# Second products of two token groups in float32, and a later split of w_out

## The chip, the cores and the metric

The kernel runs on one core of a Trainium2 chip. Its engines work side by side: TensorE (PE, matmuls, with its weight loads shown apart as PEld), VectorE (DVE), ScalarE (ACT), GpSimd (POOL) and SyncE (SP, which here only issues transfers). The metric is the device time of one execution in microseconds. The kernel before took 1150.65 us, the median of three runs (1146.93 to 1151.56).

## The reference

Attention with a causal mask and a bias from cumulative sums, for 8 batches of 8 heads, 576 positions, head dimension 64; then a gated feed-forward layer over the 4608 tokens of 512 numbers:

```python
scores = scale * np.matmul(q, k.transpose(0, 1, 3, 2))
cum = np.cumsum(np.maximum(s, 0.0), axis=-1)
bias = -(cum[:, :, :, None] - cum[:, :, None, :])
scores = np.where(causal, -1e9, scores + np.minimum(bias, 0.0))
attn = softmax(scores);  x = (attn @ v), heads side by side   # 4608 x 512
gate = 1.0 / (1.0 + np.exp(-(x @ w_gate)))                    # w_gate, w_val: 512 x 1536
out = (gate * (x @ w_val)) @ w_out                            # w_out: 1536 x 512
```

The weights arrive as 64-bit floats and are decoded on the chip to float32.

## The kernel before

Most products are made of float16 halves: each operand is scaled by a power of two and split into a high and a low half, and a product is the three passes high x high, high x low and low x high, added up in PSUM.

**Attention** goes head by head, five row tiles a head; one tile is a tick of the main loop (320 ticks). Scores are made on PE, bias and row bound on DVE (L529), the exponential on ACT (L530), the split of the result on ACT and DVE (L534, L539, L547), then DMA transposes it, and PE multiplies with v (L562 to L567). After each pair of heads the result is split and transposed into the tokens x of one batch. The first eight heads are done in float32, scores and product with v alike (L631, L662).

**The feed-forward layer** takes tokens in 18 groups of GT = 256 and the 1536 hidden columns in NF = 12 blocks f of 128. A unit (g, f) is `ffn_in`: 24 passes for gate and value (L714), the tanh on ACT (L719), and the gated product on DVE (L721). `ffn_mid` scales the product by `hsc` and splits it (L729 on ACT, L730 on DVE). `ffn_out` adds for both row tiles of 128 tokens the product with block f of w_out (L745, 512 columns) in PSUM, over f from 0 to 11, and after the last block copies the sum out with a scale (L764) and stores it (L765).

**The first two groups** are special. Their 24 units are issued in program order at ticks 44 to 51, while weights are still being decoded, and their gated products are kept in float32 (`t2first`, in the large buffer `t2big`). The scale `hsc` needs the sizes of all blocks of w_gate and of w_out, so their `ffn_mid` and `ffn_out` come only after `hidden_scale`, behind all 24 units.

**Weights** come in 18 steps: 12 for the blocks of w_gate and w_val, 6 for pairs of blocks of w_out. A step loads, decodes (L298 to L301), bounds the columns with a small matmul (L310, L313), makes a power-of-two scale `wscale` (L332, L334) and splits into halves (L337 on ACT, L338 on DVE). `invw` is the inverse of the scale. The halves of w_out lie in `w2all`, whose room also serves as raw room for loads.

**The last two groups** use fewer products: `tail_weights` builds sums of weight blocks (L787 to L795) in the rooms `troom`, `tail_tokens` sums of tokens, and `tail_pair` makes both groups' hidden values from seven half-depth products (L833), with copies and sums on ACT and DVE between (L846 to L864). Their `ffn_out` follow one block behind; those of block 11 come last, each row tile evacuated in halves by ACT and DVE (L755, L757).

**Order.** A planner fixes each engine's order of instructions before the run, from priorities (mostly program order), data dependencies and its own estimate of durations. On the chip each engine runs that order and waits where a dependency is late. Attention has raised priority (`first`) from tick 44 to 87, so weight steps, units and products of the first two groups fill what it leaves. From tick 87 on, units and attention are interleaved in program order; a group's units can start when all heads of its batches are done, and its `ffn_out` run LAG = 3 units behind.

Of the kernel before, what the change touches and what calls it, by code (L numbers as in the profile page):

```python
# [18 lines left out]
P = 128  # L19
GT = 256  # L20
# [5 lines left out]
def tile_attention_then_gated_ffn(  # L26
# [60 lines left out]
    w1 = [cp.tile([P, NC, 2, 2, P], F16, name=f"w1_{f}") for f in range(NF)]  # L87

    w2all = cp.tile([P, NF // 2, 2, 8, 2, DM // 8], F16, name="w2all")
    w2 = [w2all[:, f // 2, :, :, f % 2] for f in range(NF)]  # L90
    e_s = [cp.tile([P, n * P], F32, name=f"e_{i}") for i, (_, _, n) in enumerate(SETS)]
    p_s = [cp.tile([P, 2, n * P], F16, name=f"p16_{i}") for i, (_, _, n) in enumerate(SETS)]

# [39 lines left out]
    wscale = cp.tile([P, 2, NF], F32, name="wscale")  # L133
    hsc = cp.tile([P, NF], F32, name="hsc")
    gmax = cp.tile([P, 1], F32, name="gmax")
    cum_d = dp.tile([NH, S], F32, name="cum_d")

    def pin(ins):
# [177 lines left out]
    def split_weight(n, a, m):  # L316

        o, f = wsteps[n]
        if o:
            hi, lo = (w2all[:, f // 2, l].rearrange("p h x n -> p (h x n)") for l in range(2))  # L320
        else:
            a = a.rearrange("p (c n) -> p c n", n=P)
            hi, lo = (w1[f].rearrange("p c g l n -> p (c g) l n")[:, :, l] for l in range(2))
        if m is None:
            ss = wp.tile([P, 1], F32, tag="wss", name=f"wss{n}")
            nc.scalar.activation(hi, a, AF.Square, accum_out=ss)
            tot = wp.tile([P, 1], F32, tag="wst", name=f"wtot{n}")
            nc.gpsimd.partition_all_reduce(tot, ss, P, ADD_REDUCE)
            pow2_of(wscale[:, o, f : f + 1 + o], tot, f"w{n}", 204 if o else 202)
        else:  # L330
            e = wp.tile([P, 1], I32, tag="xe", name=f"xe_w{n}")
            nc.vector.tensor_scalar(e, column_bound(n, m).bitcast(I32), 0x7F800000, None, ALU.bitwise_and)  # L332
            dst = wscale[:, o, f : f + 1 + o]
            nc.vector.tensor_scalar(dst.bitcast(I32), e.to_broadcast([P, 2]) if o else e, -1.0,  # L334
                                    (268 if o else 266) * 2.0 ** 23, ALU.mult, ALU.add)
        sc = wscale[:, o, f : f + 1]
        nc.scalar.activation(hi, a, AF.Copy, scale=sc)  # L337
        nc.vector.scalar_tensor_tensor(lo, a, sc, hi, ALU.mult, ALU.subtract)  # L338

    def inverse_weights(o, fs):  # L340
        inverse_pow2(invw[:, o, fs], wscale[:, o, fs])

    def hidden_scale():


        inverse_weights(1, slice(0, NF))
        g = wp.tile([P, NF], F32, tag="hsg", name="hsg")
        nc.vector.tensor_tensor(g, invw[:, 0], invw[:, 1], ALU.mult)
        m = wp.tile([P, 1], F32, tag="hsm", name="hsm")
        nc.vector.tensor_reduce(m, g, mybir.AxisListType.X, ALU.max)  # L350
        nc.vector.tensor_scalar(gmax, m, 2.0 ** -100, None, ALU.max)
        r = wp.tile([P, 1], F32, tag="hsr", name="hsr")
        nc.vector.reciprocal(r, gmax)
        nc.vector.tensor_scalar(hsc, g, r, 2.0 ** -13, ALU.mult, ALU.mult)
        out_scale(0)

    osc = {}
# [347 lines left out]
    def ffn_in(g, f):  # L705
        pcs, n = pieces_of(g)
        ps = pp.tile([P, 2, GT], F32, tag="gv", name=f"gv{g}_{f}")
        for gv in range(2):
            for a, e, b in pcs:
                c0 = PAD + g * GT - b * S  # L710
                c = 0
                for cc in range(NC):
                    for wl, xl in ((0, 0), (0, 1), (1, 0)):
                        nc.tensor.matmul(ps[:, gv, a:e], w1[f][:, cc, gv, wl], x_of(b, cc)[:, xl, c0 + a : c0 + e],  # L714
                                         start=(c == 0), stop=(c == 3 * NC - 1))
                        c += 1
        th = fp.tile([P, GT], F32, tag="th", name=f"th{g}_{f}")
        for a, e, b in pcs:
            nc.scalar.activation(th[:, a:e], ps[:, 0, a:e], AF.Tanh, scale=scb[b][:, f : f + 1])  # L719
        t2 = t2first[g * NF + f] if g < 2 else fp.tile([P, GT], F32, tag="t2", name=f"t2_{g}_{f}")  # L720
        nc.vector.scalar_tensor_tensor(t2[:, :n], th[:, :n], 1.0, ps[:, 1, :n], ALU.add, ALU.mult)  # L721
        t2s[g, f] = t2
        if g > 1:
            ffn_mid(g, f)

    def ffn_mid(g, f):
# [5 lines left out]

    def ffn_out(g, f, tiles=range(GT // P), last=False):
        pcs, n = pieces_of(g)
        if g < 2:
            ffn_mid(g, f)
        h = hst[g, f]
        for tt in tiles:
            m = min(P, n - tt * P)
            if f == 0:  # L740
                tag = ("x", "av")[tt] if g == NG - 1 else "o"
                ops_[g, tt] = pp.tile([P, 512], F32, tag=tag, name=f"o{g}_{tt}", **({} if tag == "o" else {"bufs": 1}))
            ps = ops_[g, tt]
            for c, (hl, wl) in enumerate(((0, 0), (0, 1), (1, 0))):
                nc.tensor.matmul(ps[:m], h[:, hl, tt * P : tt * P + m], w2[f][:, wl],  # L745
                                 start=(f == 0 and c == 0), stop=(f == NF - 1 and c == 2))
            if f == NF - 1:
                i = (g * GT // P + tt) % 2
                o = rows_out[:, i * DM : (i + 1) * DM] if g < NG - 1 else last_rows(tt)
                if last:  # L750

                    b = pcs[-1][2]
                    rows = out[g * GT + tt * P : g * GT + tt * P + m, :]
                    w = DM // 2
                    nc.scalar.activation(o[:m, :w], ps[:m, :w], AF.Copy, scale=osc[b][:m])  # L755
                    nc.scalar.dma_start(rows[:, :w], o[:m, :w])
                    nc.vector.tensor_scalar(o[:m, w:], ps[:m, w:], osc[b][:m], None, ALU.mult)  # L757
                    nc.sync.dma_start(rows[:, w:], o[:m, w:])
                    del ops_[g, tt]
                    continue  # L760
                for a, e, b in pcs:
                    a, e = max(a - tt * P, 0), min(e - tt * P, P)
                    if a < e:
                        nc.scalar.activation(o[a:e], ps[a:e], AF.Copy, scale=osc[b][a:e])  # L764
                nc.gpsimd.dma_start(out[g * GT + tt * P : g * GT + tt * P + m, :], o[:m])  # L765
                del ops_[g, tt]

# [8 lines left out]
    G1, G2 = NG - 2, NG - 1  # L776
    GX = PAD + G1 * GT - (B - 1) * S
    TS, Sx = {}, {}
    troom = [t2big[:, i * 4 * GT : (i + 1) * 4 * GT] for i in range(6)]
    troom += [e_s[1][:, : 4 * GT], p_s[1].rearrange("p l n -> p (l n)").bitcast(F32)[:, : 4 * GT]]  # L780

    def tail_weights(f):
# [14 lines left out]

    def tail_tokens():

        a = t2big[:, 4 * 4 * GT : 6 * 4 * GT].rearrange("p (k c n) -> p k c n", k=4, n=GT)  # L800
        for k in range(4):
            for c in range(2):
                x_ = x_of(B - 1, 2 * (k % 2) + c)[:, :, GX + (k // 2) * GT : GX + (k // 2 + 1) * GT]
# [14 lines left out]
    def tail_pair(f):  # L818
# [10 lines left out]
        def product(ps, ws, xs, first_):  # L829
            c = 0  # L830
            for cc in range(NC // 2):
                for wl, xl in ((0, 0), (0, 1), (1, 0)):
                    nc.tensor.matmul(ps, ws[:, cc, wl], xs[cc][:, xl], start=first_ and c == 0, stop=c == 3 * NC // 2 - 1,  # L833
                                     skip_group_check=True)
                    c += 1

        ga = pp.tile([P, 2, GT], F32, tag="gv", name=f"ta{f}")[:, 0]
        un = pp.tile([P, 2, GT], F32, tag="gv", name=f"tu{f}")[:, 0]
# [13 lines left out]
        nc.vector.tensor_tensor(u2, un, one, ALU.add)  # L852
        product(ga, w[:, hi, 0], x(G1, 1), False)
        product(vd[:, 0], w[:, hi, 1], s(1), False)
        product(vd[:, 1], t[:, hi, 0], x(G2, 1), False)
        nc.vector.tensor_tensor(v2, five[:, 0], five[:, 1], ALU.add)
        nc.vector.tensor_tensor(v2, v2, u2, ALU.add)
        nc.vector.tensor_tensor(v1, vd[:, 0], u2, ALU.add)
# [1 line left out]
        for g, gate, val in ((G1, ga, v1), (G2, g2, v2)):  # L860
            th = fp.tile([P, GT], F32, tag="th", name=f"th{g}_{f}")
            nc.scalar.activation(th, gate, AF.Tanh, scale=scb[B - 1][:, f : f + 1])
            t2 = fp.tile([P, GT], F32, tag="t2", name=f"t2_{g}_{f}")
            nc.vector.scalar_tensor_tensor(t2, th, 1.0, val, ALU.add, ALU.mult)  # L864
            t2s[g, f] = t2
            ffn_mid(g, f)

    units = [(g, f) for g in range(NG) for f in range(NF)]
    state = {"u": 0, "o": 0}
# [29 lines left out]
    for n in range(nticks + 12):  # L899
# [146 lines left out]
        if n >= NE and state["u"] < 2 * NF:  # L1046
# [13 lines left out]
            if state["u"] == 2 * NF:  # L1060
                hidden_scale()
                while state["o"] < 2 * NF:
                    emit_out()
                late_slots()
        if (n - 30) % (NTL * H) == 0 and n >= 30 + NTL * H:
            ffn_scale((n - 30) // (NTL * H))
# [7 lines left out]
            while state["u"] < min(want, len(units)):  # L1074
                emit_unit()
    rest = len(units) - 2 * NF
    for f in range(4):
        tail_weights(f)
    tail_tokens()
    for f in range(4, len(troom)):  # L1080
        tail_weights(f)
    with first():
        while state["u"] < rest:
            emit_unit()
    for f in range(NF):
        tail_pair(f)
        while state["o"] < rest:
            emit_out()
        if f:
            ffn_out(G1, f - 1)  # L1090
            ffn_out(G2, f - 1)
        if f + len(troom) < NF:
            tail_weights(f + len(troom))
    for g in (G1, G2):
# [30 lines left out]
```

## Time and profile before

| | us |
|---|---|
| median of three runs | 1150.65 (1146.93 to 1151.56) |
| the profiled execution | 1149.97 |
| its span, first to last instruction | 1148.2 |
| PE busy in the span | 1092.8 (95%) |
| DVE busy | 828.9 (72%) |
| ACT busy | 753.4 (66%) |
| POOL busy | 203.1 (18%) |
| products with w_out (L745), 1296 matmuls, PE busy | 315.2 |

The profile is of one execution. A row of instructions gives start or count, busy time, the mean of one in nanoseconds, and the idle time of the engine just before, with what ended it. PE's ends are modelled and overlap from one matmul to the next, so spacing from start to start is the better measure of a matmul's cost. A row can carry several shapes.

### The profile page before, as it was taken

How to read it: one execution, taken by the hardware profiler on the slowest of the kernel's cores; microseconds unless marked ns; L12 is line 12 of the kernel's file. 1: busy time of each engine (PE TensorE's matmuls, PEld its weight loads, DVE VectorE, ACT ScalarE, POOL GpSimd, SP SyncE). 2: the span in 40 equal slices, each digit the busy share in tenths (PEclk: the TensorE clock that was granted, in tenths of full speed). 3: DMA queues.
4: the chain of work that ended last, by engine and by line, in shares of the span. 5: the costliest groups of instructions: out<-in, count | busy, mean ns of one | idle time of the engine just before them, and what ended most of it. 6: DMA issues, size and time to landing. Idle time of an engine off the chain costs nothing.

```text
span 1148.2 us, 30316 instructions
## 1 busy us (share of the span) xinstructions
PE 1092.8 (95%) x11796; PEld 856.6 (75%) x11796; DVE 828.9 (72%) x2360; ACT 753.4 (66%) x1475; POOL 203.1 (18%) x471
## 2 busy tenths in 40 slices
PE   6997868989999999999999999999999999999997
PEld 4776757747777787788777777778877787787775
DVE  6868979866787687766565567777777779673854
ACT  6878657767786777676656577767776766343433
POOL 3311101022232222221111122222221213000000
PEclk9999989999999999999999999999999999999999
DMA  9767886998989698875736468878877664100001
GB/s 281 226 183 140 195 151 142 179 182 166 172 170 174 156 177 162 154 151 116 170 66 149 99 156 162 162 156 169 165 146 158 142 118 95 23 20 11 10 1 37
DMA packets 445933, 157.62 MB, mean 137 GB/s; under 512 B 403615, under 2 KB 436383, under 8 KB 445790
## 3 DMA queue, kind: packets, MB, share of 16 engines
q1 hardware_dynamic: 418974, 127.64, 56.7%
q10 hardware_dynamic: 23616, 17.30, 5.2%
q0 software_dynamic: 3200, 10.75, 2.6%
q8 instruction: 92, 1.51, 0.5%
q14 instruction: 51, 0.42, 0.1%
HBM read 56.92 MB, written 9.58 MB: 58 GB/s over the span
## 4 chain that ended last, share of the span: by engine, by line
PE 70%; DMA 9%; DVE 7%; ACT 5%; issue 5%; SPq 2%; POOL 1%; ACTq 0%; DVEq 0%; POOLq 0%
PE gv L714 34%; PE o L745 20%; DMA v<-in_v_dram 3%; PE s L491 3%; PE tv L833 3%; PE s L489 3%; DMA T<-qk 1%; PE ta L833 1%; PE av L564 1%; DMA w2all<-in_moe_w_out_dram 1%; PE av L562 1%; DVE e L529 1%; PE av L563 1%; PE na_ps L662 1%; SPq L463 1%
## 5 line engine op out<-in xcount | busy, mean ns | idle before, releaser
L714 PE MATMUL gv<-x,w 128*128 128x256 f16 (+3 forms) x6336 | 555.6, 245 | 10.1 <-DVE t2f L721 6.7
L714 PEld LDWEIGHTS <-w 128*128 128x128 f16 x6336 | 481.7, 99 | 63.6 <-issue 11.7
L745 PE MATMUL o<-w2all,h 128*128 128x512 f16 x1296 | 315.2, 379 | 3.6 <-ACT h L729 3.5
L530 ACT ACTIVATE e<-e,em 128x576 f32<-128x576 f32 x280 | 153.3, 557 | 90.3 <-DVE em L529 87.5
L745 PEld LDWEIGHTS <-h 128*128 128x128 f16 x1296 | 123.2, 98 | 110.3 <-ACT h L729 5.2
L511 POOL TENSOR_SCALAR_AFFINE_SELECT rl<-rl 128x128 f32<-128x128 f32 (+1 forms) x240 | 89.7, 374 | 501.9 <-DVE em L529 460.1
L529 DVE CUSTOM_DVE_ANT_0 e<-s,rl,qkcf 128x576 f32<-128x576 f32 x280 | 151.3, 544 | 32.7 <-PE s L491 17.0
L729 ACT ACTIVATE h<-t,hsc 128x256 f16<-128x256 f32 x192 | 96.6, 503 | 91.0 <-DVE t L721 89.0
L719 ACT ACTIVATE th<-gv,scb 128x256 f32<-128x256 f32 (+3 forms) x264 | 99.1, 403 | 66.3 <-PE gv L714 59.0
L539 DVE SCALAR_TENSOR_TENSOR p<-e,p 128x384 f16<-128x384 f32 x224 | 102.9, 498 | 40.0 <-ACT p L534 38.3
L721 DVE SCALAR_TENSOR_TENSOR t<-th,gv 128x256 f32<-128x256 f32 x168 | 69.7, 415 | 63.8 <-ACT th L719 63.8
L730 DVE SCALAR_TENSOR_TENSOR h<-t,hsc,h 128x256 f16<-128x256 f32 x192 | 93.4, 487 | 28.7 <-ACT h L729 26.3
L534 ACT ACTIVATE p<-e 128x1152 f16<-128x1152 f32 x112 | 112.0, 1001 | 2.8 <-DMA pt<-p 0.3
L489 PE MATMUL s<-T 128*128 128x288 f16 (+2 forms) x246 | 63.8, 277 | 8.0 <-DMA T<-qk 4.1
L562 PE MATMUL av<-v,pt 128*128 128x65 f16 x560 | 67.6, 193 | 2.0 <-DMA pt<-p 2.0
L451 POOL PARTITION_BROADCAST cr<-cr x63 | 59.4, 950 | 56.8 <-DMA cr<-cum_d 33.2
L563 PE MATMUL av<-v,pt 128*128 128x64 f16 x560 | 67.6, 192 | 0.0
L564 PE MATMUL av<-v,pt 128*128 128x65 f16 x560 | 67.6, 194 | 0.0
L491 PE MATMUL s<-T 128*128 128x288 f16 (+2 forms) x246 | 61.5, 277 | 4.3 <-DMA T<-T 4.3
L562 PEld LDWEIGHTS <-pt 128*128 128x128 f16 x560 | 52.5, 97 | 7.8 <-DMA pt<-p 2.9
L563 PEld LDWEIGHTS <-pt 128*128 128x128 f16 x560 | 52.5, 97 | 4.5
L564 PEld LDWEIGHTS <-pt 128*128 128x128 f16 x560 | 52.7, 97 | 0.2
(210 smaller groups left out, 1542.4 us busy)
## 6 DMA issues: line engine op xcount, KB each, us to landing
v<-v SPq DMA_DIRECT2D x56, 162.5 KB
v<-in_v_dram SPq DMA_DIRECT2D x64, 128.0 KB
out_dram<-io POOLq DMA_DIRECT2D x32, 256.0 KB, 3.4
T<-T SPq DMA_DIRECT2D x82, 72.0 KB
t2f<-in_v_dram SPq DMA_DIRECT2D x20, 288.0 KB
qk<-in_q_dram SPq DMA_DIRECT2D x17, 288.0 KB
qk<-in_k_dram SPq DMA_DIRECT2D x17, 288.0 KB
w2all<-in_moe_w_gate_dram ACTq DMA_DIRECT2D x7, 512.0 KB
```

The source lines that it names most:

```text
L489: nc.tensor.matmul(ps[:, : b_ - a], lhs, T[i][:, 0, a:b_], start=True, stop=False)
L529: nc.vector.tensor_tensor_reduce(e, ps, r, c, MASKED, ALU.add, ALU.min, acc)
L530: nc.scalar.activation(e_t[t][:, :w], e_t[t][:, :w], AF.Exp, bias=acc, scale=-1.0)
L534: nc.scalar.activation(p_s[h_][:, 0], e_s[h_], AF.Copy, scale=PSCALE)
L539: nc.vector.scalar_tensor_tensor(flat[:, LOW[t] * P : (LOW[t] + t) * P], e_t[t][:, : t * P], PSCALE, flat[:, kb * P : (kb + t) * P], ALU.m ...
L562: nc.tensor.matmul(AV[i][:, t], hi, v_[:, D : 2 * D + 1], start=kb == 0, stop=False)
L563: nc.tensor.matmul(AV[i][:, t, 0:D], hi, v_[:, 0:D], start=False, stop=False)
L564: nc.tensor.matmul(AV[i][:, t], lo, v_[:, D : 2 * D + 1], start=False, stop=False)
L714: nc.tensor.matmul(ps[:, gv, a:e], w1[f][:, cc, gv, wl], x_of(b, cc)[:, xl, c0 + a : c0 + e], start=(c == 0), stop=(c == 3 * NC - 1))
L719: nc.scalar.activation(th[:, a:e], ps[:, 0, a:e], AF.Tanh, scale=scb[b][:, f : f + 1])
L729: nc.scalar.activation(h[:, 0], t2, AF.Copy, scale=hsc[:, f : f + 1])
L745: nc.tensor.matmul(ps[:m], h[:, hl, tt * P : tt * P + m], w2[f][:, wl], start=(f == 0 and c == 0), stop=(f == NF - 1 and c == 2))
```

## The change

For the first two groups `ffn_mid` is left out. The float32 gated product goes into the matmul as it is, against w_out in float32: one float32 matmul for each block and row tile in place of three float16 ones.

In a step of w_out, the split is replaced by two ACT copies in float32 (one for each of the two blocks), each scaled by `share`, the block's inverse weight scale over the largest of them. `block_shares` makes `share` once, before the first w_out step. The copies lie in `w2all`, in the place of the halves.

After the products of both groups `split_out` makes the float16 halves of w_out from these copies, two blocks at a time: ACT makes the high half, DVE the low half. The first pair goes to a part of `t2big` (columns 20 GT to 24 GT), each further pair over the float32 copy of the pair before. Thereby `troom` has one room fewer (7, not 8), and `tail_tokens` uses other rooms.

At the end, the products of block 10 of the last two groups are issued after the last product of `tail_pair(11)`.

```diff
-    w2 = [w2all[:, f // 2, :, :, f % 2] for f in range(NF)]
+    w2 = {}
+    w2f = [w2all[:, j].rearrange("p l h x n -> p (l h x n)").bitcast(F32).rearrange("p (h x n) -> p x h n", h=8, x=2)
+           for j in range(NF // 2)]
...
+        if o:
+            if f == 0:
+                block_shares()
+            a = a.rearrange("p (h x n) -> p x h n", h=8, x=2)
+            for x in range(2):
+                nc.scalar.activation(w2f[f // 2][:, x], a[:, x], AF.Copy, scale=share[:, f + x : f + x + 1])
+            return
         sc = wscale[:, o, f : f + 1]
         nc.scalar.activation(hi, a, AF.Copy, scale=sc)
         nc.vector.scalar_tensor_tensor(lo, a, sc, hi, ALU.mult, ALU.subtract)
...
+    def block_shares():
+
+        inverse_weights(0, slice(0, NF))
+        nc.vector.tensor_reduce(imax, invw[:, 0], mybir.AxisListType.X, ALU.max)
+        r = wp.tile([P, 1], F32, tag="hsr", name="imr")
+        nc.vector.reciprocal(r, imax)
+        nc.vector.tensor_scalar(share, invw[:, 0], r, None, ALU.mult)
+
+    def split_out(j):
+
+        t = w2all[:, j - 1] if j else t2big[:, 20 * GT : 24 * GT].bitcast(F16).rearrange(
+            "p (l h x n) -> p l h x n", l=2, h=8, x=2)
+        for x in range(2):
+            f = 2 * j + x
+            hi, lo = (t[:, l, :, x] for l in range(2))
+            nc.scalar.activation(hi, w2f[j][:, x], AF.Copy, scale=resc[:, f : f + 1])
+            nc.vector.scalar_tensor_tensor(lo, w2f[j][:, x], resc[:, f : f + 1], hi, ALU.mult, ALU.subtract)
+            w2[f] = t[:, :, :, x]
...
+        nc.vector.scalar_tensor_tensor(resc, wscale[:, 0], imax, wscale[:, 1], ALU.mult, ALU.mult)
+        osc["f32"] = wp.tile([P, 1], F32, tag="osf", name="oscf", bufs=1)
+        nc.vector.tensor_scalar(osc["f32"], imax, sv[0][1], 0.5, ALU.mult, ALU.mult)
...
-        if g < 2:
-            ffn_mid(g, f)
-        h = hst[g, f]
+        h = hst[g, f] if g > 1 else t2first[g * NF + f]
...
-            for c, (hl, wl) in enumerate(((0, 0), (0, 1), (1, 0))):
+            if g < 2:
+                nc.tensor.matmul(ps[:m], h[:, tt * P : tt * P + m], w2f[f // 2][:, f % 2], start=f == 0, stop=f == NF - 1)
+            for c, (hl, wl) in enumerate(((0, 0), (0, 1), (1, 0)) if g > 1 else ()):
...
                 while state["o"] < 2 * NF:
                     emit_out()
+                for j in range(NF // 2):
+                    split_out(j)
...
-        if f:
-            ffn_out(G1, f - 1)
-            ffn_out(G2, f - 1)
+        with tc.issue_after(last.ins) if f == NF - 1 else ExitStack():
+            for g in (G1, G2):
+                if f:
+                    ffn_out(g, f - 1)
```

More of the change, by code (lines that the diff above doesn't have):

```diff
@@ L135, in tile_attention_then_gated_ffn @@
     gmax = cp.tile([P, 1], F32, name="gmax")
+    imax = cp.tile([P, 1], F32, name="imax")
+    share = cp.tile([P, NF], F32, name="share")
+    resc = cp.tile([P, NF], F32, name="resc")
     cum_d = dp.tile([NH, S], F32, name="cum_d")
@@ L721, in ffn_in @@
         nc.vector.scalar_tensor_tensor(t2[:, :n], th[:, :n], 1.0, ps[:, 1, :n], ALU.add, ALU.mult)
-        t2s[g, f] = t2
         if g > 1:
+            t2s[g, f] = t2
             ffn_mid(g, f)
@@ L763, in ffn_out @@
                     if a < e:
-                        nc.scalar.activation(o[a:e], ps[a:e], AF.Copy, scale=osc[b][a:e])
+                        nc.scalar.activation(o[a:e], ps[a:e], AF.Copy, scale=osc[b if g > 1 else "f32"][a:e])
                 nc.gpsimd.dma_start(out[g * GT + tt * P : g * GT + tt * P + m, :], o[:m])
@@ L778, in tile_attention_then_gated_ffn @@
     TS, Sx = {}, {}
-    troom = [t2big[:, i * 4 * GT : (i + 1) * 4 * GT] for i in range(6)]
+    troom = [t2big[:, i * 4 * GT : (i + 1) * 4 * GT] for i in range(5)]
     troom += [e_s[1][:, : 4 * GT], p_s[1].rearrange("p l n -> p (l n)").bitcast(F32)[:, : 4 * GT]]
@@ L798, in tail_tokens @@
     def tail_tokens():
-        a = t2big[:, 4 * 4 * GT : 6 * 4 * GT].rearrange("p (k c n) -> p k c n", k=4, n=GT)
+        a = t2big[:, 3 * 4 * GT : 5 * 4 * GT].rearrange("p (k c n) -> p k c n", k=4, n=GT)
         for k in range(4):
@@ L832, in product @@
                 for wl, xl in ((0, 0), (0, 1), (1, 0)):
-                    nc.tensor.matmul(ps, ws[:, cc, wl], xs[cc][:, xl], start=first_ and c == 0, stop=c == 3 * NC // 2 - 1,
-                                     skip_group_check=True)
+                    last = nc.tensor.matmul(ps, ws[:, cc, wl], xs[cc][:, xl], start=first_ and c == 0,
+                                            stop=c == 3 * NC // 2 - 1, skip_group_check=True)
                     c += 1
+            return last
         ga = pp.tile([P, 2, GT], F32, tag="gv", name=f"ta{f}")[:, 0]
@@ L854, in tail_pair @@
         product(vd[:, 0], w[:, hi, 1], s(1), False)
-        product(vd[:, 1], t[:, hi, 0], x(G2, 1), False)
+        last = product(vd[:, 1], t[:, hi, 0], x(G2, 1), False)
         nc.vector.tensor_tensor(v2, five[:, 0], five[:, 1], ALU.add)
@@ L866, in tail_pair @@
             ffn_mid(g, f)
+        return last
     units = [(g, f) for g in range(NG) for f in range(NF)]
@@ L1076, in tile_attention_then_gated_ffn @@
     rest = len(units) - 2 * NF
-    for f in range(4):
+    for f in range(3):
         tail_weights(f)
     tail_tokens()
-    for f in range(4, len(troom)):
+    for f in range(3, len(troom)):
         tail_weights(f)
@@ L1085, in tile_attention_then_gated_ffn @@
     for f in range(NF):
-        tail_pair(f)
+        last = tail_pair(f)
         while state["o"] < rest:
             emit_out()
-        if f:
-            ffn_out(G1, f - 1)
-            ffn_out(G2, f - 1)
+        with tc.issue_after(last.ins) if f == NF - 1 else ExitStack():
+            for g in (G1, G2):
+                if f:
+                    ffn_out(g, f - 1)
         if f + len(troom) < NF:
```

## The prediction

> **What bounds the kernel now.** I read the page first, for the engines' shares, then the windows, to see where TensorE (PE) is not full, then the waits of PE in that stage.
>
> ```profile
> PE 1092.8 (95%) x11796; PEld 856.6 (75%) x11796; DVE 828.9 (72%) x2360; ACT 753.4 (66%) x1475; POOL 203.1 (18%) x471
> ```
>
> ```profile
> 262.00:1133.00 871.00, 865.56 (x9796) 680.14 (x9795) 612.58 (x1749) 557.43 (x1109) 157.81 (x375) 1.00 0.61 124
> 160.00:180.00 20.00, 16.81 (x163) 13.46 (x163) 13.00 (x26) 7.08 (x11) 2.41 (x4) 0.83 1.03 190
> 180.00:200.00 20.00, 16.43 (x180) 13.65 (x177) 19.54 (x59) 19.55 (x34) 1.79 (x3) 1.00 0.63 132
> 200.00:220.00 20.00, 17.40 (x192) 15.19 (x192) 17.06 (x62) 13.09 (x26) 0.73 (x3) 1.00 1.04 201
> 220.00:240.00 20.00, 17.71 (x169) 10.92 (x169) 17.02 (x51) 15.06 (x31) 3.26 (x7) 1.00 0.74 142
> 240.00:260.00 20.00, 18.36 (x136) 9.88 (x137) 12.47 (x37) 13.72 (x27) 4.63 (x11) 1.00 0.92 186
> ```
>
> The columns of a window are its length, then busy time of PE, weight load, DVE, ACT and POOL, the granted clock, the DMA share and GB/s. From 262 to 1133 us PE has 865.56 of 871.00 us: there the time is PE's work and nothing else. From 160 to 260 us it is idle for 3.19, 3.57, 2.60, 2.29 and 1.64 us, 13.3 us in all. In this stage w_out is decoded and split and the first two token groups are multiplied, behind attention. So I count end time as PE work plus PE idle time: added PE work costs its full length unless it lands in idle time, and relief of DVE or ACT is worth only the PE idle time it removes.
>
> **The products: three float16 passes become float32.** For two groups, 12 blocks and two row tiles there are 48 sums; before, each takes three 512-column matmuls (144), after it one float32 matmul. The trace has no 512-column float32 matmul; it has shorter ones and the float16 ones.
>
> ```profile
> 64.70 1.19 PE L631 MATMUL s<-nk,nq 128*128 128x288 f32 x4
> 65.73 0.22 PE L518 MATMUL s<-above,eye 128*128 128x128 bf16 x1
> 65.78 0.97 PE L631 MATMUL s<-nk,nq 128*128 128x448 f32 x2
> 66.59 0.22 PE L518 MATMUL s<-above,eye 128*128 128x128 bf16 x1
> ```
>
> ```profile
> 265.13 2.75 PE L745 MATMUL o<-w2all,h 128*128 128x512 f16 x12
> 267.72 0.19 PE L491 MATMUL s<-T 128*128 128x64 f16 x1
> ```
>
> ```profile
> L631 PEld LDWEIGHTS s<-nk,nq 128*128 128x128 f32 x96 | 16.5, 208 | 6.3 <-issue 2.5 <-DVE em L643 2.2
> ```
>
> Twelve float16 products take 267.72 - 265.13 = 2.59 us from start to next start, 0.216 each, so 144 take 31.1 us. One float32 matmul shows as two instructions: the pair of 448 columns takes 66.59 - 65.78 = 0.81 us, and two pairs of 288 take 65.73 - 64.70 = 1.03 us, 0.515 each. A float16 pass of 288 columns would be 0.216 x 288/512 = 0.1215 us, four of them 0.486; the row is 0.029 above. So float32 is four passes and a little. For 512 columns the low end is 4 x 0.216 = 0.864 us; the high end is the line through the two rows, 0.81 + 64 x (0.81 - 0.515)/160 = 0.93. I take 0.864 + 0.029 = 0.893, the value by the longer run: 48 x 0.893 = 42.9 us, **+11.8 us** of PE work (+10.4 to +13.5). Each float32 weight load takes 0.208 us, under the 0.43 us of the instruction before it, and I cost it at nothing.
>
> The Trainium skill speaks against that last step: "TensorE: Matmul & The Clock Gate", Part 3, The mechanism, says that a weight load overlaps a running matmul only if it goes to another row group, and here all loads fill the whole array; by that rule the sum would gain the loads, the fourth rival below. The trace disagrees with it for float16, where the run of twelve above has no room for its loads.
>
> **Work taken off ACT and DVE.**
>
> ```profile
> L338 DVE SCALAR_TENSOR_TENSOR w2all<-wa,wscale,w2all 128x1024 f16<-128x1024 f32 x3 | 3.8, 1279 | 0.6 <-ACT w2all L337 0.6
> L338 DVE SCALAR_TENSOR_TENSOR w2all<-io,wscale,w2all 128x1024 f16<-128x1024 f32 x3 | 3.8, 1276 | 0.1
> L337 ACT ACTIVATE w2all<-io,wscale 128x1024 f16<-128x1024 f32 x3 | 3.4, 1141 | 1.2 <-DVE xe_w L332 1.2
> L729 ACT ACTIVATE h<-t2f,hsc 128x256 f16<-128x256 f32 x24 | 11.2, 497 | 2.8 <-PE o L745 2.7
> L730 DVE SCALAR_TENSOR_TENSOR h<-t2f,hsc,h 128x256 f16<-128x256 f32 x24 | 11.1, 488 | 2.7 <-ACT h L729 2.7
> L764 ACT ACTIVATE io<-o,osc 128x512 f32<-128x512 f32 x28 | 18.6, 679 | 0.8 <-PE o L745 0.7
> L539 DVE SCALAR_TENSOR_TENSOR p<-e,p 128x512 f16<-128x512 f32 x56 | 38.8, 693 | 0.0
> 159.83 0.21 DVE L377 TENSOR_SCALAR scb<-invw,vin 128x12 f32<-128x12 f32 x1
> ```
>
> The six w_out blocks lose their low half (DVE 7.6 us); their ACT copy of 1.14 becomes two of 512 columns, by the evacuation row 0.679 each, so ACT gains 6 x 0.22 = 1.3 us. The 24 splits of the gated product go: ACT 11.2, DVE 11.1 us. New are block_shares (four operations on 12 columns at most, 0.21 each: 0.8 us of DVE) and two more small ones in hidden_scale. None of this is PE work. Its worth is PE idle time that these operations caused:
>
> ```profile
> 183.89 1.28 DVE L338 SCALAR_TENSOR_TENSOR w2all<-io,wscale,w2all 128x1024 f16<-128x1024 f32 x1
> 185.96 0.30 PE L489 MATMUL s<-T 128*128 128x320 f16 x1 [1.20 <-DVE em L529]
> 191.04 2.78 PE L714 MATMUL gv<-x,w 128*128 128x256 f16 x24 [0.61 <-DVE t2f L721]
> 200.97 0.30 PE L491 MATMUL s<-T 128*128 128x288 f16 x1 [1.91 <-DMA T<-T]
> 220.15 1.04 PE L745 MATMUL o<-w2all,h 128*128 128x512 f16 x4 [1.78 <-ACT h L729]
> 240.42 0.20 PE L562 MATMUL av<-v,pt 128*128 128x65 f16 x1 [1.19 <-DMA pt<-p]
> ```
>
> At 185.96 PE waits for the row bound that stands right behind a w_out split on DVE; at 191.04 for a gated product behind the next one. With two splits of 1.28 us gone from a window where DVE is busy 19.54 of 20, the transpose awaited at 200.97 can be sent up to 2.5 us earlier. At 220.15 PE waits for the first split product, which no longer exists, and float32 products need no ACT or DVE, so they can stand in for 240.42. I credit all five: **-6.7 us**. Bounds: nothing (the order of each engine is fixed ahead, and a stall on a late transfer stays if nothing is put before it) and the whole idle time of the stage (second rival). block_shares' 0.8 us is hidden by the DVE time freed; without that cover it would cost 0.8.
>
> **What moves later.** split_out adds 12 copies on ACT (12 x 0.679 = 8.1 us) and 12 subtractions on DVE (12 x 0.693 = 8.3 us). Its first block goes into room that still holds gated products of group 1, so it waits for that group's last matmul; each further block goes over the block before. Behind it wait the products of group 2. One block takes copy, copy, subtraction: 0.68 + 0.68 + 0.69 = 2.05 us.
>
> ```profile
> 277.06 1.46 PE L745 MATMUL o<-w2all,h 128*128 128x512 f16 x6
> ...
> 281.22 1.46 PE L745 MATMUL o<-w2all,h 128*128 128x512 f16 x6
> ```
>
> Group 1's last product ends at 267.72 and group 2's first starts at 277.06, then one per 4.2 us, so a pair of blocks is wanted every 8.3 us and made in 2.05. The cover is 9.3 us of first products and attention: cost 0. If the cover is gone it is 2.05 us once, or up to 4 with attention's operations between; below nothing it cannot go. Evacuation of the first groups uses another scale of the same shape; no transfer is added, and none passes another on SP's, ACT's or POOL's queue.
>
> **The tail.** The weight sums get seven rooms, not eight, so one build moves into the loop of the last two groups.
>
> ```profile
> 1070.00:1080.00 10.00, 10.00 (x75) 7.18 (x74) 9.18 (x20) 4.71 (x10) 0.00 (x0) 1.00 0.01 2
> L787 DVE TENSOR_TENSOR tw<-w 128x1024 f32<-128x1024 f16 x12 | 14.6, 1219 | 0.1
> L789 DVE TENSOR_TENSOR tw<-tw 128x256 f32<-128x256 f32 x12 | 5.0, 418 | 0.0
> L795 DVE TENSOR_TENSOR t2f<-tw,t2f 128x1024 f16<-128x1024 f32 x10 | 12.2, 1219 | 1.2 <-ACT t2f L794 1.2
> ```
>
> ```profile
> 1133.89 1.47 PE L833 MATMUL tv<-tx,t2f 128*128 128x256 f16 x12 [0.41 <-DVE tn L859]
> 1135.20 2.32 PE L745 MATMUL o<-w2all,h 128*128 128x512 f16 x10
> 1135.50 0.57 ACT L847 COPY tc<-tv 128x512 f32<-128x512 f32 x1
> 1140.68 2.76 PE L745 MATMUL o<-w2all,h 128*128 128x512 f16 x12 [1.42 <-ACT h L729]
> ```
>
> A build is DVE work of 1.22 + 4 x 0.42 + 1.22 = 4.1 us. Where such builds run already, DVE is busy 9.18 of 10 us and PE still 10.00, so a fifth costs nothing; without that cover, what it asks beyond DVE's free time, 4.1 us at most. At the end, the products of block 10 move behind the last product of block 11. Twelve of them, 2.59 us, then cover the chain that leaves PE idle for 1.42 us. But ten of them now fill the time of the copy that ends at 1136.07; without them PE may wait from the end of the first half, 1133.89 + 12 matmuls, about 1135.2, to 1136.07. So the gain lies between 1.42 and 1.42 - 0.87 = 0.55; I take **-0.7**, near the low end, since the other first halves of block 11 have run by then.
>
> **Sum.** +11.8 - 6.7 - 0.7 = +4.4 us. The profiled execution took 1149.97 us (span 1148.2, 1.8 around it), which becomes 1154.4; it lies 0.7 below the median of 1150.65, so I forecast **1155 us**, 0.4% more. About 0.5%, or 5.75 us, is what a measurement of this kernel can tell from no change (1144.9 to 1156.4).
>
> **Rivals.**
> 1. *Paid in full.* The new order keeps as many stalls, most of them on transfers (200.97, 240.42), and only the tail gains: 1150.65 + 11.8 - 0.7 = 1161.8, with one exposed first block 1163.8. For it: PE is above 17 of 20 us busy already in 200 to 260. It decides once fewer than 5.4 us come back. Chance 0.22.
> 2. *The stage closes up.* DVE and ACT had 19.54 and 19.55 of 20 us in 180 to 200; with 18.7 us less on DVE the float32 products fill what attention leaves open. All 13.3 us of idle time from 160 on and the 3.28 us ahead of it come back:
>
> ```profile
> 159.95 4.12 PE L714 MATMUL gv<-x,w 128*128 128x256 f16 x24 [3.28 <-DVE t2f L721]
> ```
>
>    1150.65 + 11.8 - 16.6 - 1.4 = 1144.5. Against it: 160 to 180, where DVE had 13.00 and ACT 7.08 of 20 us, was no shortage of these engines. Chance 0.24.
> 3. *The passes were hidden anyway.* Group 2 needs batch 1's tokens, which come late; if PE waits for them, the extra passes land there, while stalls shrink a little: about 1150. Against it: from 220 on PE is nearly full. Chance 0.09.
> 4. *Float32 weight loads are exposed.* 96 x 0.208 = 20 us on top: 1175. Against it: in the run of four at 64.70, 0.2575 us per instruction leave only 0.0145 beside its two passes of 0.1215. Chance 0.03.
>
> **How the numbers follow.** The forecast has 0.42; its own range is 1151 to 1160, from the term of the passes (10.4 to 13.5) and of the stalls (3 to 9), and a third of it (0.14) lies above 1156.4. Rival 2 is faster in 0.18 and within the bound in 0.06, rivals 1 and 4 are slower, rival 3 is within. Faster 0.18, same 0.28 + 0.06 + 0.09 = 0.43, slower 0.14 + 0.22 + 0.03 = 0.39. The range, 1143 to 1164, holds the two main rivals' times and leaves out their far ends and rival 4.
>
> **What would show it.** Float32 matmuls of w_out in 96 instructions, spaced 0.43 to 0.47 us; 0.6 us or more means exposed loads. The idle time of PE between 160 and 275 us should fall from about 13 to about 7. The first float32 product should start before 220. No PE wait on ACT or DVE of split_out ahead of group 2's first product. One PE wait of under a microsecond near the end in place of 1.42. The forecast is wrong if idle time does not fall (then 1162) or falls by more than 12 us, or if the stretch after 280 us, full before, shows gaps.

## The result, and the profile after

The changed kernel takes 1159.37 us (median of six runs, 1157.62 to 1161.1) against 1149.65 us for the kernel before beside it (six runs, 1146.93 to 1151.56). The ratio is 1.0095, interval 1.0081 to 1.0110: slower by 0.8 to 1.1%. A second set of six runs, on another occasion, gave 1.0117 (1.0087 to 1.0147). The forecast was 1155 us, 0.4% more. The time lies in the stated range, 4.4 us above the forecast and 2.4 us below the first rival's 1161.8; the likeliest of the three cases, a change too small to tell from none, did not come.

The profiled execution of the changed kernel took 1159.94 us, with a span of 1158.2, 10.0 above that of before. The busy line of its page:

```profile
PE 1104.9 (95%) x11748; PEld 860.6 (74%) x11748; DVE 824.8 (71%) x2348; ACT 752.9 (65%) x1469; POOL 202.9 (18%) x471
```

PE is busy 12.1 us longer (1104.9 - 1092.8) and idle 2.1 us less (1158.2 - 1104.9 = 53.3, before 1148.2 - 1092.8 = 55.4). The sum of the prediction had +11.8 and -7.4. So the added work came, and most of the idle time stayed.

Most line numbers used here are 34 higher in the changed kernel: units are L748 (gate and value) and L755 (gated product), float32 products L777, float16 products L779, the copies of w_out L346, `split_out` L370 (ACT) and L371 (DVE), the evacuation L798, the products of the last two groups L867. The float32 products and their weight loads, from the groups by shape, and the products from the timeline of PE:

```profile
L777 PE MATMUL o<-w2all,t2f 128*128 128x512 f32 x96 | 42.3, 594 | 0.1
L777 PEld LDWEIGHTS o<-w2all,t2f 128*128 128x128 f32 x96 | 17.9, 190 | 20.5 <-issue 19.6 <-ACT io L798 0.3 <-ACT w2all L346 0.2
```

```profile
195.76 8.80 PE L777 MATMUL o<-w2all,t2f 128*128 128x512 f32 x20
204.39 1.25 PE L748 MATMUL gv<-x,w 128*128 128x256 f16 x10
```

Twenty instructions take 204.39 - 195.76 = 8.63 us, 0.4315 each; a float32 matmul is two of them, 0.863 us. 48 make 41.4 us against 31.1 before: +10.3. The first stands at 195.76, where the first float16 product of before stood at 220.15. Now the stage, up to the first product of group 2 (277.06 us before, 287.13 after), in windows with the prediction's columns, first before, then after:

```profile
139.00:196.00 57.00, 45.20 (x487) 37.63 (x485) 49.54 (x138) 39.86 (x66) 4.68 (x7) 0.94 0.76 151
196.00:277.00 81.00, 73.53 (x735) 51.16 (x733) 62.26 (x189) 56.72 (x114) 12.75 (x31) 1.00 0.85 172
160.00:277.00 117.00, 103.71 (x1046) 75.86 (x1046) 90.80 (x263) 79.80 (x150) 16.78 (x36) 0.97 0.85 171
```

```profile
139.00:196.00 57.00, 45.85 (x498) 38.70 (x495) 48.85 (x139) 40.79 (x70) 5.26 (x8) 0.91 0.75 153
196.00:287.00 91.00, 86.35 (x722) 57.66 (x721) 56.04 (x177) 54.31 (x102) 17.40 (x30) 1.00 0.81 158
160.00:287.00 127.00, 113.36 (x1009) 80.35 (x1007) 84.20 (x253) 79.58 (x143) 20.39 (x35) 0.97 0.82 162
287.00:1143.00 856.00, 849.42 (x9597) 666.78 (x9595) 607.48 (x1728) 550.00 (x1093) 150.75 (x369) 1.00 0.66 123
```

```profile
287.13 1.46 PE L779 MATMUL o<-t2f,h 128*128 128x512 f16 x6
```

The whole 10 us have arisen by 287 us; behind it both kernels take 871.1 us to the end. DVE was relieved as forecast (62.26 of 81 us before, 56.04 of 91 after), and PE's idle time from 139 us on fell from 11.8 + 7.5 = 19.3 to 11.2 + 4.7 = 15.8 us. From 160 us on, where the prediction looked for a fall from about 13 to about 7, it did not fall: 117.00 - 103.71 = 13.3 us before, 127.00 - 113.36 = 13.6 after. PE's busy time from 139 us on grew by more than the passes, 0.7 + 12.8 = 13.5 us. Two things on record go with that: 46 fewer of PE's instructions lie ahead of 139 us (888, before 934), so some work comes later, as an early lag below shows; and the granted clock between 139 and 196 us was 0.91, before 0.94, which over 57 us is an estimated 1.7 us of work. What PE waited for between 85 and 340 us, before and then after (us in total, times, longest; some rows left out):

```profile
PE gv L714 <- DVE t2f L721: 6.7, 5, 3.3
PE s L491 <- DMA T<-T: 4.3, 3, 1.9
PE s L489 <- DMA T<-qk: 4.1, 3, 3.0
...
PE gv L714 <- DVE wscale L334: 2.1, 1, 2.1
...
PE o L745 <- ACT h L729: 1.8, 1, 1.8
```

```profile
PE gv L748 <- DVE t2f L755: 9.6, 5, 3.2
PE s L523 <- DMA T<-qk: 6.4, 4, 3.1
...
PE s L525 <- DMA T<-T: 2.8, 4, 1.1
```

The wait on the split product (1.8) is gone, as the change intends. The one on the weight scale (2.1, at 149.55 us) is gone from the list, but at 152.95 us PE waits 2.12 us for a gated product instead. In all, the waits on gated products rose from 6.7 to 9.6 and those on transposed queries and keys from 4.1 to 6.4. All rows of these two answers add up to 30.7 us before and 28.8 after.

### The profile page after: what moved, and what is told of

Read it like the earlier page. It is cut to its first block, busy times and chain, and to the rows that moved or that the text cites. A ratio compares the mean times of both kernels' runs of the same rounds, so it can differ in the third digit from the quotient of the medians.

```text
span 1158.2 us, 30185 instructions
## 1 busy us (share of the span) xinstructions
PE 1104.9 (95%) x11748; PEld 860.6 (74%) x11748; DVE 824.8 (71%) x2348; ACT 752.9 (65%) x1469; POOL 202.9 (18%) x471
## 4 chain that ended last, share of the span: by engine, by line
PE 67%; issue 8%; DMA 7%; DVE 7%; ACT 5%; SPq 2%; POOL 2%; ACTq 0%; POOLq 0%; DVEq 0%
PE gv L748 31%; PE o L779 18%; DMA v<-in_v_dram 3%; PE tv L867 3%; PE s L525 2%; DMA T<-qk 2%; PE s L523 2%; PE o L777 2%; PE s L665 2%; PE na_ps L696 1%; PE ta L867 1%; DVE e L563 1%; POOL rl L545 1%; SPq L497 1%; PE av L598 1%
## 5 line engine op out<-in xcount | busy, mean ns | idle before, releaser
L748 PE MATMUL gv<-x,w 128*128 128x256 f16 (+3 forms) x6336 | 553.4, 245 | 11.3 <-DVE t2f L755 9.6
L748 PEld LDWEIGHTS <-w 128*128 128x128 f16 x6336 | 480.1, 98 | 64.3 <-issue 14.6
L779 PE MATMUL o<-w2all,h 128*128 128x512 f16 x960 | 233.8, 379 | 0.0
L779 PEld LDWEIGHTS <-h 128*128 128x128 f16 x1152 | 109.7, 98 | 92.8 <-ACT h L763 0.6
L563 DVE CUSTOM_DVE_ANT_0 e<-s,rl,qkcf 128x576 f32<-128x576 f32 x280 | 151.2, 544 | 28.9 <-PE s L525 11.6
L755 DVE SCALAR_TENSOR_TENSOR t<-th,gv 128x256 f32<-128x256 f32 x168 | 69.6, 415 | 59.3 <-ACT th L753 59.2
```

The source lines that it names most:

```text
L563: nc.vector.tensor_tensor_reduce(e, ps, r, c, MASKED, ALU.add, ALU.min, acc)
```

## The experiments

Times are medians; the ratio is to the kernel before in the same set of runs, with its interval. "Place" is how far the large tiles (x, v, the transposed queries and keys, and everything else made after the small scales) have moved against the kernel before, in bytes of a partition, worked out from the sizes of the small tiles; where a tile starts in memory is in no trace. The time of a 2600-byte packet (the 56 writes of v, `v<-v`) is its mean over 3584 packets of the trace.

| kernel | place | ratio | us | 2600-byte packet, ns |
|---|---|---|---|---|
| before | 0 | 1 | 1148 to 1150 | 167 |
| after | 160 | 1.0095 (1.0081 to 1.0110) | 1159.37 | 195 |
| after, again (x10) | 160 | 1.0117 (1.0087 to 1.0147) | 1163.55 | 194 |
| late split (x4) | 160 | 1.0110 (1.0086 to 1.0134) | 1160.22 | 193 |
| after, padded (x6) | 256 | 1.0092 (1.0077 to 1.0107) | 1158.86 | 169 |
| three passes (x2) | 160 | 1.0045 (1.0029 to 1.0061) | 1153.17 | 189 |
| three passes, padded (x8) | 256 | 1.0015 (1.0000 to 1.0031) | 1150.30 | 170 |
| tail alone (x3) | 0 | 0.9990 (0.9972 to 1.0009) | 1146.61 | 166 |
| fourth pass (x1) | 0 | 1.0167 (1.0126 to 1.0209) | 1164.96 | 166 |
| fourth pass, shifted (x9) | 160 | 1.0198 (1.0173 to 1.0222) | 1171.79 | 192 |
| shift by 160 (x5) | 160 | 1.0067 (1.0045 to 1.0088) | 1154.77 | 192 |
| shift by 256 (x7) | 256 | 0.9999 (0.9981 to 1.0018) | 1148.69 | 169 |
| shift by 64 (x11) | 64 | 1.0050 (1.0028 to 1.0071) | 1155.23 | 193 |

**Added PE work alone (x1).** The kernel before, with a fourth float16 pass for groups 0 and 1:

```diff
-            for c, (hl, wl) in enumerate(((0, 0), (0, 1), (1, 0))):
+            passes = ((0, 0), (0, 1), (1, 0)) + (((1, 1),) if g < 2 else ())
+            for c, (hl, wl) in enumerate(passes):
...
```

> The kernel before with a fourth float16 pass (low half by low half) in the products of the first two groups, and nothing else: 48 more matmuls of 512 columns, 48 x 0.216 = 10.4 us of PE work, about what float32 adds (96 instructions spaced 0.4315 us are 41.4 us against 31.1). Passes theory (PE work is paid in full, whatever ACT and DVE do): about 10 us above the kernel before, 1159 to 1161. Rival, hidden passes (products of this stage fit into idle time of PE, and the loss lies in the later split): at most 3 us above it, 1150 to 1153.

Measured: 1.0167, 17.1 us by the medians and 19.2 by the ratio, for 48 x 0.216 = 10.4 us of PE work. The median is also above the 1159 to 1161 us expected. Nothing of the work is hidden in this stage, so the third rival, *the passes were hidden anyway*, falls. The profiled execution, the second fastest of the kind, is 10.0 us behind before at 331 us, 10.7 at 950 and 12.9 in its span (1161.0); why the added work costs more than its own length here is not settled.

**The change without added PE work (x2).** Three bfloat16 passes stand for the float32 matmul:

```diff
-                nc.tensor.matmul(ps[:m], h[:, tt * P : tt * P + m], w2f[f // 2][:, f % 2], start=f == 0, stop=f == NF - 1)
...
+                for c in range(3):
+                    nc.tensor.matmul(ps[:m], h16, w16, start=f == 0 and c == 0, stop=f == NF - 1 and c == 2)
```

> The changed kernel with three bfloat16 passes over the upper halves of the float32 numbers in place of each float32 product of the first two groups (the result of these two groups is left out: it is not their product). Everything else as changed: no split of the gated product, w_out split later. PE work is that of the kernel before, so the run shows what the relief of ACT and DVE is worth alone. Passes theory: 10 us below the changed kernel, 1148 to 1150, so the relief is worth 0 to 1.5. My forecast's credit of 6.7 us for five stalls: 1142 to 1144. Blocked queue theory (the first split holds ACT and DVE while the last products run): stays above 1152.

Measured: 1.0045. This kernel has all that the change takes off ACT and DVE, the early copies, the late split and the tail, and as much PE work as before. By the prediction's credits it should be 7.4 us faster than before; it is 3 to 7 us slower, in the range that the theory of a blocked queue gave (above 1152). So something in the change costs time beside its passes.

**The tail alone (x3).** The kernel before, with the products of block 10 issued behind the last product of the tail, and nothing else of the change.

> The kernel before with the tail's edit alone: the products of block 10 of the last two groups are issued behind the last product of block 11. Seen in the changed kernel's trace: the first half of block 11 starts 10.47 us later than before and the end comes 10.0 later, a gain of 0.5. Every theory: 0.5 us below the kernel before in the last 15 us of the profile, less than the median can tell; a gain of 1.4 would say that the copy between the halves costs nothing.

Measured: 0.9990, not to be told from no change. In the profile the end, from the first half of block 11, is the same as in the changed kernel:

```profile
1130.49 1.47 PE L833 MATMUL tv<-tx,t2f 128*128 128x256 f16 x12 [0.41 <-DVE tn L860]
1132.72 0.81 PE L833 MATMUL tv<-tx,w 128*128 128x256 f16 x6 [0.76 <-ACT tc L848]
1133.37 0.82 PE L833 MATMUL tv<-x,t2f 128*128 128x256 f16 x6
1134.03 5.34 PE L745 MATMUL o<-w2all,h 128*128 128x512 f16 x24
```

The wait of 1.42 us is gone and one of 0.76 on the copy stands in its place. From the first row to the end it takes 1144.1 - 1130.49 = 13.6 us, in the changed kernel 1158.2 - 1144.36 = 13.8, before 1148.2 - 1133.89 = 14.3.

**The late split (x4).** In the trace of the changed kernel `split_out` is issued while the float32 products still run, and the in-order queues of ACT and DVE stand behind it. From the timeline:

```profile
253.57 20.87 PE L777 MATMUL o<-w2all,t2f 128*128 128x512 f32 x48
...
271.05 1.33 ACT L370 ACTIVATE t2f<-w2all,resc 128x512 f16<-128x512 f32 x2 [13.42 <-PE o L777]
...
274.55 1.41 DVE L371 SCALAR_TENSOR_TENSOR t2f<-w2all,resc,t2f 128x512 f16<-128x512 f32 x2 [15.93 <-ACT io L798]
```

ACT stands for 13.42 us and DVE for 15.93, which the prediction had not seen. To try whether this is the cost, x4 splits each pair of w_out one pair ahead of group 2's products with it:

```diff
+        if g == 2 and f % 2 == 0:
+            for j in range(f // 2 + (f > 0), min(f // 2 + 2, NF // 2)):
+                split_out(j)
...
-                for j in range(NF // 2):
-                    split_out(j)
```

> The changed kernel, with each pair of blocks of w_out split only just ahead of group 2's products with it in program order (one pair ahead), not right behind the products of the first groups. Blocked queue theory: ACT (13.4 us) and DVE (15.9 us) no longer stand still for the first split, attention goes on, and the time falls by 3 to 5 us, to 1154 to 1156. Passes theory: PE had work all the while, so the time stays within 1.5 us of the changed kernel's, 1158 to 1161.

Measured: 1.0110 (1.0086 to 1.0134), as the change itself. But x4 did not take the standing away. Its later pairs are split later (ACT at 282.50, 286.41 and 290.72 us), while the first split still holds both engines:

```profile
272.04 1.33 ACT L370 ACTIVATE t2f<-w2all,resc 128x512 f16<-128x512 f32 x2 [13.67 <-PE o L780]
...
275.54 1.41 DVE L371 SCALAR_TENSOR_TENSOR t2f<-w2all,resc,t2f 128x512 f16<-128x512 f32 x2 [16.17 <-ACT io L801]
```

So x4 says nothing of the standing. The trace of the changed kernel does: while ACT and DVE stand, PE runs 48 float32 instructions without a gap, and between 244.5 and 292.2 us it has no idle time over 0.35 us. The standing leaves no PE idle time there; no run without it was made.

**An early lag, and the addresses (x5, x6, x7).** The trace has a mark that all kernels share: the splits of v on ACT (`v<-v,vsc`, 28 of them). The first lies at 86.6 us before, 90.3 after, 91.1 in x2, 89.9 in x4, but 87.3 in x3 and 86.8 in x1. So these three kernels with the change are 3.3 to 4.5 us late when none of the changed work has begun and PE's instructions are the same. What differs this early is where tiles lie. The diff, in a part not shown above, allocates three small tiles between the scales and the large tiles:

```diff
     gmax = cp.tile([P, 1], F32, name="gmax")
+    imax = cp.tile([P, 1], F32, name="imax")
+    share = cp.tile([P, NF], F32, name="share")
+    resc = cp.tile([P, NF], F32, name="resc")
```

4, 48 and 48 bytes are rounded up to 32, 64 and 64: every tile behind them moves by 160 bytes (those behind a fourth small scale, `oscf`, by 192). x5 is the kernel before with just these lines, the tiles unused; x7 the kernel before with one unused tile of 256 bytes there; x6 the changed kernel with its four small tiles padded to 256 together.

> The kernel before, with the three small tiles of the change (imax, share, resc) allocated where the change allocates them and used by nothing: the instructions are those of before, and every tile that is allocated after gmax stands 160 bytes further on, which is no multiple of 64 bytes. Theory (addresses): the lag of 3.3 to 4.5 us that the three kernels with the change show before 90 us, with TensorE's order the same and none of the changed work begun, comes from these addresses: the first rows show it as in the changed kernel (sp_sb<-s_sb 1.4 us instead of 0.54, rel<-cum 0.97 instead of 0.51), the twelfth-group marks near 90 us lie 3 to 4.5 us late, and the time is 3 to 5 us above before (about 1152). Rival (the program's contents, or chance between runs): the rows stay at 0.5 us, the marks within 0.6 us, and the time is that of before (about 1148).

> The kernel before with one unused tile of 256 bytes at the same place, so that the same tiles move by 256 bytes: the control that tells alignment from mere movement. Theory (addresses, by alignment): as before, 1148 us within 1.5 us, sp_sb<-s_sb 0.5 us, no lag near 90 us. If any movement of the tiles costs: 3 to 5 us above before.

> The changed kernel, with its four small tiles padded so that every tile allocated after them stands 256 bytes further on than in the kernel before, where it is 160 to 192 in the changed kernel; all instructions stay. Theory (addresses): the early lag goes (marks near 90 us within 0.6 us of before), sp_sb<-s_sb is 0.5 us again, and the time falls by 3 to 5 us from that of the change, to about 1155 us, some 6 us above before, which is the float32 passes (+10.3) less what the stalls and the tail give back. Rival: as the changed kernel, 1159 us.

Measured: three unused tiles make the kernel before 0.67% slower (0.45 to 0.88), and 256 bytes change nothing. One sign of mine was wrong: `sp_sb<-s_sb` is as slow in x7 (1.33 us) as in x5 (1.35), so this row has nothing to do with the place. The transfers do, while the engines work as long in x5 as in x7 (DVE 829.9 and 830.5 us, ACT 753.2 and 754.1). From the list of DMA queues (packets, MB, share of 16 engines' span), before, after, x5, x7 and x6:

```profile
q1 hardware_dynamic: 418974, 127.64, 56.7%
```

```profile
q1 hardware_dynamic: 418974, 127.64, 60.9%
```

```profile
q1 hardware_dynamic: 418974, 127.64, 59.5%
```

```profile
q1 hardware_dynamic: 418974, 127.64, 56.6%
```

```profile
q1 hardware_dynamic: 418974, 127.64, 57.5%
```

The same packets and bytes take 651 us of each DMA engine before (0.567 x 1148.2) and 705 after (0.609 x 1158.2), 689 in x5 and 666 in x6. By size in the trace, 2600-byte packets go from 167 to 195 ns, 1152-byte ones (the copies `T<-T` and `t2f<-t2f`) from 71 to 84, the many 256-byte ones from 22 to 24 in the mean. The 2600-byte and 1152-byte packets are long in all kernels moved by 160 and short in all moved by 0 or 256. The first mark follows: 86.6 to 88.4 us with 0 or 256, 89.5 to 92.0 with 160.

But x6 was expected at 1155 and took 1158.86. Its transfers are short and its first mark is at 87.2, and yet it is 6.4 us late at the third mark (148.7 against 142.4). In the changed kernel the padding is worth 0.3 us by the first set of runs of the change (the ratios differ by 0.0003) and 2.9 by the second (0.0025). The half-widths of the intervals of these differences are 2.4 and 3.9 us, so it may be nothing, and it is a few us at most.

**Which of the two is it in the changed kernel? (x8, x9, x10).** x8 is the kernel with three passes, padded as x6; x9 is the fourth-pass kernel with the three unused tiles; x10 is the change again.

> The kernel of the run with three bf16 passes (the changed kernel with as much work on TensorE as before; the result of the first two groups is left out, since only the upper halves are multiplied), with its small tiles padded as in the aligned run, so that the big tiles stand on multiples of 64 bytes again. Theory A (the addresses are the whole of what the change costs besides its passes): 2600-byte packets 168 ns instead of 189, and 1148 us, the time of before within 1.5 us, so that the 10.8 us of the aligned changed kernel are the float32 passes alone (10.3) and nothing is refunded. Theory B (the new structure itself, with the split in the middle, costs about 5 us, whatever the addresses): 1153 us, as without the padding.

> The kernel before with a fourth float16 pass in the second products of the first two groups (as in the run with the fourth pass), with the three unused small tiles that move the later tiles by 160 bytes. Theory A (slower transfers and more work on TensorE hide each other, which is why the padding brought the changed kernel nothing): the time of the fourth-pass kernel without the shift, 1163 to 1165 us. Theory C (both are paid in full, whatever the kernel): 6 us more, about 1170 us.

> The changed kernel as it stands, on the same chip as the other two, for a comparison with its padded twin (1158.86 us, 1.0092 times before): 1159.4 us, 1.0095 times before, if the padding brings nothing; 1162 or more, if the padded twin was in fact faster by 3 us.

Measured: x8 1.0015, near theory A and far from B: 1.3 us above before by the medians and 1.7 by the ratio, where A allowed 1.5. With the transfers as before, all that the change does beside its passes is worth +1.7 us (0 to 3.6), not -7.4. Then the passes are x6 against x8: 0.0092 - 0.0015 = 0.0077, or 8.8 us, with a half-width of 2.5, which holds the 10.3 of the spacing. x9 took 1171.79, 6.8 us above x1 and near theory C, but the two were measured beside different sets of the kernel before; by their ratios the difference is 3.6 us with a half-width of 5.5, so this pair decides nothing. By ratios, the place of the tiles costs 7.8 us between x7 and x5 (half-width 3.3) and 3.4 between x8 and x2 (2.6), both clear of noise, and 0.3 or 2.9 in the changed kernel, which is not. Whether it is truly smaller there, and why, stays open. The waits of PE in x8 between 85 and 340 us show where the refund went:

```profile
PE gv L750 <- DVE t2f L757: 11.6, 7, 3.2
PE av L598 <- DMA pt<-p: 5.5, 5, 2.0
PE nx_ps L722 <- DVE x L725: 3.6, 1, 3.6
PE s L525 <- DMA T<-qk: 3.1, 2, 2.4
```

No wait on a split product is left, but those on gated products rose from 6.7 to 11.6 and those on `pt` from 2.0 to 5.5. All rows add up to 31.4 us, before 30.7. In the stretch of the five stalls that the prediction credited (6.7 us), x8 has these:

```profile
189.63 2.78 PE L750 MATMUL gv<-x,w 128*128 128x256 f16 x24 [1.31 <-DVE t2f L757]
211.78 0.20 PE L598 MATMUL av<-v,pt 128*128 128x65 f16 x1 [1.45 <-DMA pt<-p]
225.05 0.20 PE L598 MATMUL av<-v,pt 128*128 128x65 f16 x1 [1.39 <-DMA pt<-p]
239.12 0.20 PE L598 MATMUL av<-v,pt 128*128 128x65 f16 x1 [1.96 <-DMA pt<-p]
```

Of the five causes the row bound and the split product are gone, and the transpose `T<-T` holds PE for 0.25 us instead of 1.91; yet these four stalls of 6.1 us in all stand there, three of them on transfers. PE's idle time from 160 to 277 us is 117.00 - 103.93 = 13.1 us, before 13.3:

```profile
160.00:277.00 117.00, 103.93 (x1034) 75.52 (x1034) 78.31 (x242) 75.14 (x138) 17.24 (x34) 0.96 0.81 165
```

**Which multiple counts (x11).** The kernel before with an unused tile of 64 bytes.

> The kernel before with one unused tile of 64 bytes at the same place: all later tiles move by 64 bytes, between the 160 that cost about 6 us and the 256 that cost nothing. If what counts is that tiles stand on a multiple of 64 bytes: as before (1148 to 1149 us, 2600-byte packets 167 ns, transfers of queue 1 at 56.6% of the span). If what counts is the place within 256 bytes, which is the rule of the Trainium skill, "DMA: Bandwidth & Descriptors", section How a descriptor splits into AXI transactions (a descriptor that doesn't start on a multiple of 256 bytes first fetches from the multiple below it): as with 160 bytes (1153 to 1156 us, 190 ns, 59% of the span).

Measured: 1.0050, 2600-byte packets as with 160 (193 ns), and transfers of queue 1:

```profile
q1 hardware_dynamic: 418974, 127.64, 60.5%
```

So a multiple of 64 bytes isn't enough; of the places tried, only 0 and 256 are fast. That is the direction of the Trainium skill, "DMA: Bandwidth & Descriptors", How a descriptor splits into AXI transactions: a descriptor that starts off a multiple of 256 bytes first fetches from the multiple below. By its count of beats 2600 bytes would cost 84 instead of 82 when they start 64 bytes past it, an estimate of 2%; the trace has 193 against 167 ns, 16%, and it has no change for 1024-byte packets (51 and 51). The measurement decides: the four places that were tried agree with the rule, the price does not, and no run here shows where the tiles really start.

## Why the prediction was wrong

- **What bounds the kernel**: right. From 287 us on, PE has 849.42 of 856 us, and the 10.1 us by which the changed kernel is late there are 10.0 at the end.
- **The products**: mechanism right, size at the low bound. I took 0.893 us for a matmul from rows of 288 columns; it is 0.863, four passes of 0.216. The term is +10.3, not +11.8. Weight loads are hidden (rival 4 falls): 0.4315 us from start to start is two passes of 0.216, with no room for the 0.19 us that a load takes.
- **Five stalls refunded, -6.7 us**: this is the step that failed. The work did leave DVE and ACT and the wait on ACT h went, but x8 shows +1.7 us (0 to 3.6) for everything beside the passes, and PE's idle time from 160 us on stayed (13.3 us before, 13.6 after, 13.1 in x8). The waits came back elsewhere, on gated products and on transfers, with the same total. I had credited each stall as if removing what ended it would let PE run on; the next late thing stood right behind. The bound that the prediction wrote down, nothing, was close to the answer, and rival 1, *paid in full*, names this mechanism ("keeps as many stalls, most of them on transfers"). That its 1161.8 lies so near is in part luck: its passes were 1.5 us too dear, and it has no term for the place of the tiles. Rival 2, *the stage closes up*, falls: PE's idle time in the profile fell by 2.1 us, not 16.6.
- **What moves later, cost 0**: right in effect, but not by its reasons. `split_out` held ACT and DVE for 13 to 16 us, since it waits on their in-order queues for the last products. PE had 48 float32 instructions to run meanwhile and shows no idle time from it; x4, meant to test this, kept the standing.
- **The tail, -0.7**: 0.5 us in the profile, the low end, with the wait on the copy that was named.
- **Not in the sum at all**: the place of the tiles. Three small scales lengthen the transfers of queue 1 by 6% (689 us in x5 against 651, 705 in the changed kernel against 666 in x6). In the kernel before that alone is 0.45 to 0.88% of the time; in the changed kernel it is a few us at most, and the runs don't settle it further.

By the runs the sum is: the rest 1.7 (x8), passes 8.8 (x6 against x8; 10.3 by spacing), the tiles' place 0.3 or 2.9, in all 10.8 to 13.4 us, as measured (0.95 to 1.17%); they must add up, since they are steps along one chain of kernels from before to after. The shares depend on the order of the steps. With the tiles moved first, the runs give 7.7 for the place (x5), -2.5 for the rest (x2 against x5, half-width 3.1) and 5.7 to 8.3 for the passes. So a refund of some us is not excluded beside the moved tiles, but neither order leaves room for -7.4.

## What to carry to other kernels

In a stage where several resources are late in turn, the stalls that an edit removes are not its gain; credit them only where the next thing behind each stall is shown to be early, and take "none comes back" as the main case otherwise. Added work on the engine that bounds the rest of the kernel was paid in about its full length here (8.8 us, half-width 2.5, for 10.3), in x1 with more. And a new tile of a few bytes can move all tiles behind it: look at where they start, and try the small tiles padded to 256 bytes together when transfers are on the path (moved by 256 bytes, x7 shows no loss and x8 is 3.4 us faster than x2; in the changed kernel the padding brought a few us at most).

## What the runs showed of the hardware

- A float32 matmul of 512 columns costs 0.863 us from start to start, in two instructions of 0.4315, where a float16 one costs 0.216.
- With all later tiles moved by 64 or 160 bytes, 2600-byte packets took 14 to 17% longer and 1152-byte ones 13 to 19%; moved by 256 bytes they took 169 to 170 and 72 ns, before 167 and 71. 1024-byte packets did not change.
- In all profiles the stretches in which the granted clock was half lasted 3.4 us or two or three times that, but for the one at the end of each, and they differ from run to run: between 40 and 140 us the clock was 0.97 in the profile of before and 0.93 in x10, whose first mark was 4.0 us late and whose seventh, at 308 us, 19.3, where that of the same kernel's first profile was 12.9 late. Lateness early in the kernel may in part be paid twice, by the wait and by a slow clock behind it. The Trainium skill, "TensorE: Matmul & The Clock Gate", Part 1, What's actually happening, gives the same window, about 3.4 us, and idle time as the cause; no run here tells the cause apart.
